# Programs without a block, and another PSUM bank for the fifth unit of the first matmul

## The chip, the cores and the metric

The kernel runs on one core of a Trainium2 chip. A core has five engines that run their own instruction streams and meet only through semaphores: TensorE (PE, with its weight loads shown as PEld), VectorE (DVE), ScalarE (ACT), GpSimd (POOL) and SyncE (SP). SP only starts transfers and waits here; ACT also starts some. The metric is device time in microseconds for one execution. Three runs of the kernel before gave 151.83, 151.93 and 152.18, median 151.93.

## The reference

Two branches are computed on the same input x (2048 rows of 512 in bf16) and mixed by a gate for each row:

```
g = sigmoid((x * gate_w).sum(-1))
A: qkv = x @ wqkv, in 32 heads of 16
   phi(p) = [softmax(p @ w_phi), softmax(-(p @ w_phi))]      per head, for q and for k
   kv = sum over rows of phi_k^T v,   z = sum over rows of phi_k
   a = (phi_q kv / (phi_q z + 1e-6)) @ wo
B: b = relu(x @ w1) @ w2,             w1: 512 x 1376
out = g * a + (1 - g) * b
```

## The kernel before

**Layout.** All is kept in SBUF, 128 rows to a partition tile. x is needed transposed (`XT`). Its first chunk of 512 rows is loaded plain and turned by TensorE with an identity matrix (`xt..`), and ACT and DVE copy the result out of PSUM (`xe..`: `xe30` is the ACT half of the fourth tile of 128 rows); the other three chunks come through transposing DMAs.

**Branch B.** h = relu(x @ w1) is made transposed, in units `h<chunk>_<k>` of 128 of w1's columns by 512 rows: four matmuls into one PSUM bank (`pe_h`, L396). ACT then writes relu of the bank to `HT` (`rl<chunk>_<k>`, L474), and the bank is free again. The first four units of chunk 0 are made piecewise, as x arrives (`hh..`, `hr..`, L410 and L416). Later `b<m>` (L636) multiplies by w2 for each tile m of 128 rows.

**Branch A.** w_phi is folded into the weights first: `f1_0` to `f1_3` for k and `f0_..` for q are four small matmuls each (`pe_fold`, L374) that multiply the transposed wk or wq (`WT`) by a block-diagonal w_phi (`WBD`). DVE evicts `f1_0` and `f1_2` (`fe1_0`, `fe1_2`, L344), ACT the other two (L342). Then x is projected in jobs `pr_k0`, `pr_k1`, ... (L510), and DVE, POOL and ACT make the softmaxes. `a<m>` (L642) adds the A part to the PSUM bank of `b<m>`, ACT scales the sum (`oe<m>`, L687) and starts the store of it (`st<m>`, L690). The last tile is stored in two parts (L681), the second of them by SP.

**PSUM banks.** There are eight. Turning x uses banks 0 and 1 for tiles 0 and 2, and 6 and 7 for tiles 1 and 3. The four folds for k use banks 0, 1, 6, 7 (`FB`) once the turning has left them. The first four h units use banks 3, 4, 5, 2 (`GB4`), and from the fifth unit on the units go round banks 3, 4, 5 (`HB`).

**Order.** The order of the tasks on each engine is written out by hand in the table `ORDER`, one string per engine. A task waits for the tasks that it depends on through one counting semaphore per engine, and one per DMA. The lines of the table around the change are, for PE and ACT:

```
pe : ... hh3 hr0 hr1 h0_0 h0_1 h0_2 h0_3 h0_4 h0_5 f1_0 f1_1 f1_2 f1_3 h0_6 pr_k0 h0_7 h0_8 pr_k1 ...
act: ... xe30 rl0_0 rl0_1 rl0_3 rl0_2 fe1_1 fe1_3 rl0_5 rl0_4 ev_k0 rl0_8 ...
```

**The program's frame.** A block (`nc.Block()`) holds one function per engine. Entering it puts a branch into each engine's stream, and leaving it another branch to a common end. There, in a closing barrier, every engine drains and reports to POOL, POOL releases all, and each takes the release. The profile shows these instructions at L188. A like barrier at the very start (L740) stands ahead of the block, behind the setting of constants. SP's part ends with waits for the last stores to land, written at L708 and L710.

Of the kernel before, what the change touches and what calls it, by code (L numbers as in the profile page):

```python
# [27 lines left out]
    ),  # L28
    "act": (
# [119 lines left out]
def bass_gated_mix__linear_kernel_hedgehog__dense_activation_relu__prompt_kernel(  # L149
# [17 lines left out]
    NT = S // P  # L167
    ND = D // P
# [12 lines left out]
    NPH, NOM, NOT, NOS = 7, 3, 4, 5  # L181
# [6 lines left out]
    with ExitStack() as es:  # L188
        E = es.enter_context

        def sb(name, shape, dt):
            return E(nc.sbuf_tensor(name, shape, dt))
# [4 lines left out]
        WP = sb("WP", [P, 2, ND, D], BF16)  # L197
# [40 lines left out]
        def psap(off, dims):  # L238
            return ap(PS, EPS, off, dims)

        g = _Graph()
        add = g.add
# [5 lines left out]
            boost=700.0)  # L248
# [32 lines left out]
        def chunk(c):  # L281
            return slice(c * 512, (c + 1) * 512)
# [49 lines left out]
        wbd = [f"wbd{j}" for j in range(ND)]  # L332
# [7 lines left out]
        def evict(name, eng, out_, b, deps, **how):  # L340
            if eng == "act":
                add(name, eng, lambda q: q.activation(out_, PS[:, b, :], ACT.Copy), deps, dur=0.6, **how)  # L342
            else:
                add(name, eng, lambda q: q.tensor_copy(out_, PS[:, b, :]), deps, dur=0.69, **how)  # L344

        XB, FB = ((0, 1), (6, 7), (0, 1), (6, 7)), (0, 1, 6, 7)
# [7 lines left out]
        for m in range(4):  # L354
# [3 lines left out]
            for n, eng in enumerate(("act", "dve")):  # L358
                xo = XT[:, 2 * n:2 * n + 2, m * P:(m + 1) * P]
                xi = PS[:, XB[m][n], 0:2 * P].rearrange("p (j t) -> p j t", j=2)  # L360
                if eng == "act":
                    add(f"xe{m}{n}", eng, lambda q, o=xo, i=xi: q.activation(o, i, ACT.Copy), (f"xt{m}{n}",), dur=0.35,
                        boost=9000.0 - 10 * m)
                else:
                    add(f"xe{m}{n}", eng, lambda q, o=xo, i=xi: q.tensor_copy(o, i), (f"xt{m}{n}",), dur=0.37,
                        boost=9000.0 - 10 * m)
# [4 lines left out]
        HB = (3, 4, 5)  # L371
        def pe_fold(q, s, j, b):
            for i in range(ND):
                last = q.matmul(PS[:, b, i * P:(i + 1) * P], WT[:, s * ND + i, j * P:(j + 1) * P], WBD[:, i, :],  # L374
                                start=True, stop=True)
            return last

        for j in range(ND):
            b = FB[j]
            war = [f"xe{2 + j // 2}{j % 2}"]  # L380
            add(f"f1_{j}", "pe", lambda q, j=j, b=b: pe_fold(q, 1, j, b), ("wkT", *wbd, *war), dur=0.24,
                boost=1800.0)
            evict(f"fe1_{j}", ("dve", "act")[j % 2], WP[:, 1, j, :], b, (f"f1_{j}",), boost=1800.0)
        units = []
        for c in range(NC):
            units += [("h", c, k) for k in range(KT - 1)]
# [2 lines left out]
            if c == 2:  # L389
                units += [("f", 0, j) for j in range(ND)]  # L390
        freed = {b: () for b in (*HB, 2)}
        w1of = {k: (() if k < 4 else ("w1b",) if k < 8 else ("w1c",)) for k in range(KT)}

        def pe_h(q, c, k, b):
# [5 lines left out]
        def pe_h_tail(q, c, b):  # L400
            m = KREM + 1
            for n in range(4):
                for j in range(ND):
                    last = q.matmul(PS[:, b, n * m:(n + 1) * m], XT[:, j, c * 512 + n * P:c * 512 + (n + 1) * P],  # L404
                                    W1[:, j, (KT - 1) * P:(KT - 1) * P + m], start=(j == 0), stop=(j == ND - 1))
            return last
# [7 lines left out]
        def pe_h_rest(q, k, c0, c1, first):  # L414
            for j in range(ND):
                last = q.matmul(PS[:, GB4[k], c0:c1], W1[:, j, k * P:(k + 1) * P], XT[:, j, c0:c1],  # L416
                                start=(j == 0 and first), stop=(j == ND - 1), skip_group_check=True)
            return last


        GB4 = (*HB, 2)
# [3 lines left out]
        for j in range(1, ND):  # L425
            add(f"hh{j}", "pe", lambda q, j=j: pe_h_first(q, j, 0, 2 * P), (f"xe0{j // 2}", f"xe1{j // 2}", f"w1a{j}", prev), dur=0.44,
                boost=8500.0)
            prev = f"hh{j}"

        for k in range(2):  # L430
            add(f"hr{k}", "pe", lambda q, k=k: pe_h_rest(q, k, 2 * P, 3 * P, True), ("xe20", "xe21", prev), dur=0.22,
                boost=8200.0)
# [6 lines left out]
        def gate(c):  # L439

            s4 = slice(4 * c, 4 * c + 4)
            add(f"ge{c}", "act", lambda q, s4=s4: q.activation(EG[:, s4], GL[:, s4], ACT.Exp), (f"gr{c}",), dur=0.22)
            add(f"gp{c}", "act", lambda q, s4=s4: q.activation(EP[:, s4], EG[:, s4], ACT.Copy, bias=1.0), (f"ge{c}",),
                dur=0.2)
            add(f"go{c}", "dve", lambda q, s4=s4: q.reciprocal(OMG[:, s4], EP[:, s4]), (f"gp{c}",), dur=0.15)

        for n, (kind, a, k) in enumerate(units):
            b = GB4[n] if n < 4 else HB[(n - 4) % len(HB)]
            if kind == "h":
                halved = n < 4  # L450
                deps = [*xof[a], *w1of[k], prev, *freed[b]]
                if k == KT - 1:
                    deps.append("gw")
                    add(f"h{a}_{k}", "pe", lambda q, a=a, b=b: pe_h_tail(q, a, b), deps, dur=0.69)
                    prev = f"h{a}_{k}"
                    hrow = psap(b * 512, [[KREM + 1, 4], [1, KREM]])
                    add(f"rl{a}_{k}", "act", lambda q, a=a, i=hrow: q.activation(
                        HR[:, a % 2, :, 0:KREM], i, ACT.Relu), (prev, f"hx{a - 2}" if a > 1 else None), dur=0.6, boost=RL)
                    add(f"hx{a}", "sp", lambda q, a=a: q.dma_start_transpose(
                        out=HT[:, KT - 1, chunk(a)].rearrange("p (n t) -> p n t", t=P),  # L460
                        in_=HR[:, a % 2, :, :].rearrange("p n k -> p (n k)")),
                        (f"rl{a}_{k}", "hpad"), dur=1.2, lat=1.6, dma=True)
                    add(f"gr{a}", "dve", lambda q, a=a, b=b: q.tensor_scalar(
                        GL[:, 4 * a:4 * a + 4], psap(b * 512 + KREM, [[KREM + 1, 4]]), GATE_LIMIT, -GATE_LIMIT,
                        ALU.min, ALU.max), (prev, f"rl{a}_{k}"), dur=0.2, boost=500.0)
                    freed[b] = (f"rl{a}_{k}", f"gr{a}")
                    gate(a)
                    continue
                add(f"h{a}_{k}", "pe", lambda q, a=a, k=k, b=b, h=halved:
                    pe_h_rest(q, k, (3 if k < 2 else 2) * P, 4 * P, k > 1) if h else pe_h(q, a, k, b),  # L470
                    deps, dur=(0.22 if k < 2 else 0.44) if halved else 0.87,
                    boost=8000.0 if n < 3 else 0.0)
                prev = f"h{a}_{k}"
                add(f"rl{a}_{k}", "act", lambda q, a=a, k=k, b=b: q.activation(  # L474
                    HT[:, k, chunk(a)], PS[:, b, :], ACT.Relu), (prev,), dur=0.6, boost=RL)
                freed[b] = (f"rl{a}_{k}",)
            else:
                deps = ["wqT", *wbd, prev, *freed[b]]
                add(f"f{a}_{k}", "pe", lambda q, a=a, k=k, b=b: pe_fold(q, a, k, b), deps, dur=0.24, boost=1000.0)
                prev = f"f{a}_{k}"  # L480
                evict(f"fe{a}_{k}", FE, WP[:, a, k, :], b, (prev,), boost=1000.0)
                freed[b] = (f"fe{a}_{k}",)


        VLAG = 4
        widths = [2] * (NT // 2 - 1) + [1, 1]
# [7 lines left out]
        for m in range(NT):  # L494
            def add(*a, boost=20.0 * (len(widths) * 2 - m // 2 - VLAG), **how):
                return g.add(*a, boost=boost, **how)
# [18 lines left out]
        for jn, (kind, tiles) in enumerate(jobs):  # L515
            w = len(tiles)
            n = kind_n[kind]
# [34 lines left out]
            war = [(f"kv{m}" if jobs[jn - NF][0] == "k" else f"tq{m}") for m in jobs[jn - NF][1]] if jn >= NF else []  # L552
# [24 lines left out]
            else:  # L577
# [4 lines left out]
                    dur=0.11 + 0.207 * w)  # L582
# [24 lines left out]
                for m in tiles:  # L607
                    for hf in range(2):
# [10 lines left out]
                        war = [f"o{u0 // 2}_{u0 % 2}"] if u0 >= 0 else [f"ve{NT - 1}"]  # L619
# [26 lines left out]
                    war = [f"oe{m - len(AB)}"] if m >= len(AB) else [f"ve{NT - 1}"] if ab == 2 else list(freed[ab])  # L646
                    if m == NT - 1:
# [15 lines left out]
                        for h2 in range(2):  # L663
                            b, cs = hb[h2], cols[h2]
# [12 lines left out]
                            else:  # L677
                                add(f"oe{m}_1", "dve", lambda q, m=m, b=b, cs=cs: q.tensor_scalar(
                                    OSB[:, m % NOS, cs], PS[:, b, 0:cs.stop - cs.start], OMG[:, m:m + 1], None, ALU.mult), need,
                                    dur=0.4)  # L680
# [14 lines left out]
        order = g.schedule()  # L695
        g.number(order)
        sems = {e: nc.alloc_semaphore(f"s_{e}") for e in ENGINES}
        for t in g.tasks.values():
            if t.dma:
                sems[t.sem] = nc.alloc_semaphore(f"d_{t.name}")  # L700
        block = E(nc.Block())

        @block.sync
        def _(q):
            g.emit("sp", q, order, sems)

            for m in range(NT - NOS - 2, NT - 1):
                q.wait_ge(sems[f"st{m}"], 16)  # L708
            for hf in range(2):
                q.wait_ge(sems[f"st{NT - 1}_{hf}"], 16)  # L710

        @block.gpsimd
        def _(q):
            g.emit("pool", q, order, sems)

        @block.scalar
        def _(q):
            g.emit("act", q, order, sems)

        @block.vector  # L720
        def _(q):
            g.emit("dve", q, order, sems)

        @block.tensor
        def _(q):
            g.emit("pe", q, order, sems)


# [26 lines left out]
```

## Time and profile before

| | |
|---|---|
| timed runs | 151.83, 151.93, 152.18 us (median 151.93) |
| profiled execution, its own time | 150.82 us |
| its span, first to last instruction | 148.9 us (148.94) |
| time around the span | 1.88 us |
| PE busy | 144.6 us, 97% |
| DVE, POOL, ACT busy | 111.0, 109.6, 91.9 us |
| granted TensorE clock | 1.0 |
| last store issued by SP | at 146.73, landing 1.7 us later |

A profile comes from one execution. The timed runs are other executions, and the profiled one was 1.11 us shorter than their median. In the lines of the profile, times are microseconds from the start of the span; L636 is line 636 of the kernel; `PS<-W,HT` is output and inputs by the program's names; `[0.83 <-PE PS L416]` is the idle time of the engine before the group and what ended it. A `q` behind an engine's name marks its sequencer: semaphore, branch, drain and DMA-issuing instructions, which don't count as busy. In the rows of one source line, `17/22/28, 147.2 to 147.2` are the shortest, median and longest duration in ns, and the first and last start in us. Matmuls are pipelined, so that one's row (379 ns) is longer than the distance between two starts (216 ns), and a few matmul rows are missing from the trace.

### The profile page before, as it was taken

To read this page: it belongs to the slowest core of one execution; us is meant where nothing else is said; L and a number is where in the kernel's file an instruction comes from. 1 tells how busy PE (TensorE), PEld (TensorE's weight loads), DVE (VectorE), ACT (ScalarE), POOL (GpSimd) and SP (SyncE) were. 2 spreads that over 40 slices of the span, in tenths; PEclk is the share of its full clock that TensorE was granted. 3 is DMA by queue.
4 is the path that set the end of the run, shared out by engine and by line. 5 is a ranking of instruction groups with operands and counts; after the bars stand their busy time and mean duration, and the time that the engine had idled before them with its cause. 6 is when DMAs were issued, how large, how long until landed. Compare 5 with 4: busy or idle time off the path is not lost.

```text
span 148.9 us, 2614 instructions
## 1 busy us (share of the span) xinstructions
PE 144.6 (97%) x992; PEld 75.3 (51%) x1009; DVE 111.0 (74%) x168; ACT 91.9 (62%) x127; POOL 109.6 (74%) x72
## 2 busy tenths in 40 slices
PE   7999999999999999999999999999999999999992
PEld 2874444445654475445444554455544454455461
DVE  2532667999896948989999997999999969436301
ACT  3457769799969767898983927366565551310151
POOL 4000599999999999999999999999999791240000
DMA  4999999920030001000000191649677585966552
GB/s 149 302 205 190 220 215 193 349 71 4 12 61 0 0 4 37 0 4 0 0 0 0 36 147 35 141 106 142 153 160 198 128 213 106 143 171 146 51 167 69
DMA packets 46364, 16.11 MB, mean 108 GB/s; under 512 B 39856, under 2 KB 46352, under 8 KB 46352
## 3 DMA queue, kind: packets, MB, share of 16 engines
q1 hardware_dynamic: 43616, 13.50, 43.5%
q10 hardware_dynamic: 2736, 2.45, 5.3%
q8 instruction: 8, 0.13, 0.4%
q14 instruction: 4, 0.03, 0.1%
HBM read 4.41 MB, written 2.10 MB: 44 GB/s over the span
## 4 chain that ended last, share of the span: by engine, by line
PE 96%; ACT 1%; issue 1%; DVE 0%
PE PS L636 24%; PE PS L396 21%; PE PS L510 18%; PE PS L490 9%; PE PS L642 9%; PE PS L571 3%; PE PS L614 3%; PE PS L404 2%; PE PS L258 2%; PE PS L657 2%; PE PS L410 1%; PE PS L374 1%; PE PS L350 1%; ACT HT L474 1%; PE PS L668 1%
## 5 line engine op out<-in xcount | busy, mean ns | idle before, releaser
L550 POOL TENSOR_TENSOR TS<-PB,MX 128x1024 bf16<-128x1024 bf16 (+1 forms) x18 | 30.9, 1722 | 14.3 <-DVE MX L541 14.3
L557 DVE TENSOR_REDUCE ZB<-FT 128x128 f32<-128x2048 bf16 (+1 forms) x18 | 36.6, 2032 | 1.8 <-ACT FT L555 1.8
L636 PE MATMUL PS<-W,HT 128*128 128x512 bf16 (+1 forms) x160 | 37.5, 379 | 0.3
L555 ACT ACTIVATE FT<-TS 128x2048 bf16<-128x2048 bf16 (+1 forms) x18 | 30.9, 1718 | 8.7 <-POOL TS L550 8.5
L396 PE MATMUL PS<-XT,W 128*128 128x512 bf16 x141 | 34.3, 379 | 0.2
L550 POOL TENSOR_TENSOR TS<-MN,PB 128x1024 bf16<-128x1024 bf16 (+1 forms) x18 | 30.9, 1724 | 0.8 <-DVE MN L543 0.8
L510 PE MATMUL PS<-WP,XT 128*128 128x512 bf16 x124 | 29.9, 379 | 0.2
L564 POOL TENSOR_TENSOR FT<-FT,SC 128x2048 bf16<-128x2048 bf16 (+1 forms) x9 | 29.5, 3288 | 0.0
L474 ACT ACTIVATE HT<-PS 128x512 bf16<-128x512 f32 x40 | 22.6, 597 | 5.5 <-PE PS L396 4.6
L636 PEld LDWEIGHTS PS<-W,HT 128*128 128x128 bf16 (+1 forms) x165 | 15.5, 98 | 17.1
L541 DVE TENSOR_REDUCE MX<-PB 128x64 bf16<-128x1024 bf16 (+1 forms) x18 | 19.5, 1085 | 6.0 <-ACT PB L537 6.0
L687 ACT ACTIVATE OSB<-PS,OMG 128x512 bf16<-128x512 f32 x15 | 10.2, 687 | 22.3 <-PE PS L642 22.2
L543 DVE TENSOR_REDUCE MN<-PB 128x64 bf16<-128x1024 bf16 (+1 forms) x18 | 19.3, 1084 | 3.2 <-ACT PB L537 3.2
L396 PEld LDWEIGHTS PS<-XT,W 128*128 128x128 bf16 x144 | 13.8, 98 | 15.3
L537 ACT ACTIVATE PB<-PS 128x1024 bf16<-128x1024 f32 (+1 forms) x18 | 16.7, 927 | 6.8 <-PE PS L510 3.7
L510 PEld LDWEIGHTS PS<-WP,XT 128*128 128x128 bf16 x128 | 12.0, 98 | 13.6 <-DVE WP L344 0.4
L587 POOL TENSOR_TENSOR FT<-FT,SR 128x1024 bf16<-128x1024 bf16 (+1 forms) x9 | 15.6, 1739 | 0.7
L490 PE MATMUL PS<-WV,XT 128*128 128x512 bf16 x61 | 15.8, 379 | 0.2
L642 PE MATMUL PS<-WO,OT 128*128 128x512 bf16 x58 | 14.3, 379 | 0.1
L623 DVE SCALAR_TENSOR_TENSOR OTM<-PS,EG,RD 128x256 bf16<-128x256 f32 x32 | 13.8, 463 | 0.4 <-DVE RD L621 0.2
L621 DVE RECIPROCAL RD<-PS 128x16 f32<-128x16 f32 x32 | 6.4, 232 | 8.9 <-PE PS L614 8.7
L499 ACT ACTIVATE VS<-PS 128x512 bf16<-128x512 f32 x16 | 9.6, 602 | 4.3 <-PE PS L490 4.3
(54 smaller groups left out, 104.9 us busy)
## 6 DMA issues: line engine op xcount, KB each, us to landing
out_dram<-OSB ACTq DMA_DIRECT2D x15, 128.0 KB, 2.1
W<-in_B_w_dram SPq DMA_DIRECT2D x1, 1280.0 KB, 7.0
W<-in_B_w_dram SPq DMA_DIRECT2D x1, 512.0 KB, 5.1
WV<-in_A_wqkv_dram SPq DMA_DIRECT2D x1, 512.0 KB, 4.5
WO<-in_A_wo_dram SPq DMA_DIRECT2D x1, 512.0 KB, 7.4
FT<-in_A_x_dram SPq DMA_DIRECT2D x3, 128.0 KB, 3.7
W<-in_B_w_dram SPq DMA_DIRECT2D x1, 352.0 KB, 3.7
W<-in_B_w_dram ACTq DMA_DIRECT2D x2, 128.0 KB, 3.5
```

Source lines behind the costliest of these rows:

```text
L396: last = q.matmul(PS[:, b, :], W1[:, j, k * P:(k + 1) * P], XT[:, j, chunk(c)], start=(j == 0), stop=(j == ND - 1))
L474: add(f"rl{a}_{k}", "act", lambda q, a=a, k=k, b=b: q.activation(HT[:, k, chunk(a)], PS[:, b, :], ACT.Relu), (prev,), dur=0.6, boost=RL)
L490: last = q.matmul(PS[:, 2, :], XT[:, j, m * P:(m + 1) * P], WV[:, j, :], start=(j == 0), stop=(j == ND - 1))
L510: last = q.matmul(PS[:, n, :], XT[:, j, m * P:(m + 1) * P], WP[:, s, j, :], start=(j == 0), stop=(j == ND - 1))
L541: add(f"mx_{J}", "dve", lambda q, sl=sl, w=w, i=pbg: q.tensor_reduce(MX[:, sl, 0:w * H], i, AX.X, ALU.max), (f"ev_{J}", old("t1")), dur=0. ...
L543: add(f"mn_{J}", "dve", lambda q, sl=sl, w=w, i=pbg: q.tensor_reduce(MN[:, sl, 0:w * H], i, AX.X, ALU.min), (f"ev_{J}", old("t2")), dur=0. ...
L550: add(f"{tn}_{J}", "pool", lambda q, o3=o3, a3=a3, b3=b3: q.tensor_tensor(o3, a3, b3, ALU.subtract), (f"{'mx' if sg == 0 else 'mn'}_{J}", ...
L555: add(f"ex_{J}", "act", lambda q, fs=fs, ts=ts, w=w: q.activation(FT[:, fs, 0:w * F], TS[:, ts, 0:w * F], ACT.Exp), (f"t1_{J}", f"t2_{J}", ...
L557: add(f"sm_{J}", "dve", lambda q, fs=fs, sl=sl, w=w: q.tensor_reduce(ZB[:, sl, 0:2 * w * H], FT[:, fs, 0:w * F].rearrange("p (g d) -> p g ...
L564: add(f"nm_{J}", "pool", lambda q, f3=f3, sl=sl, w=w: q.tensor_tensor(f3, f3, SC[:, sl, 0:2 * w * H].unsqueeze(2).to_broadcast([P, 2 * w * ...
L636: last = q.matmul(PS[:, ab, :], HT[0:r, k, m * P:(m + 1) * P], W2[0:r, k, :], start=(k == 0), stop=False)
L642: last = q.matmul(PS[:, ab, :], OT[:, m % NOT, t, :], WO[:, t, :], start=False, stop=(t == ND - 1))
```

## The change

Two things are changed.

First, the block is gone. The tasks of each engine are emitted straight into the main program, and so the branch into the block, the branch out of it and the closing barrier aren't there. SP's waits for the last stores stay, and are its last instructions.

Second, unit `h0_4` writes bank 6 in place of bank 3. It now waits for `xe30`, which empties that bank of x, and no longer for `rl0_0`. The fold `f1_2`, which uses the same bank next, waits for `rl0_4`; for that `rl0_4` is moved ahead of `fe1_1` on ACT. The definition of the folds moves down in the text, since it now refers to `rl0_4`; the order of PE's tasks is the same. `h0_7`, the next unit on bank 3, waits for `rl0_0` and not for `rl0_4`.

```diff
     "act": (
-        "x01 w1a1 w1a3 xe00 xe10 xe20 xe30 rl0_0 rl0_1 rl0_3 rl0_2 fe1_1 fe1_3 rl0_5 rl0_4 ev_k0 rl0_8 rl0_6 "
+        "x01 w1a1 w1a3 xe00 xe10 xe20 xe30 rl0_0 rl0_1 rl0_3 rl0_2 rl0_4 fe1_1 fe1_3 rl0_5 ev_k0 rl0_8 rl0_6 "
...
         freed = {b: () for b in (*HB, 2)}
+        freed[FB[2]] = ("xe30",)
...
-            b = GB4[n] if n < 4 else HB[(n - 4) % len(HB)]
+            b = GB4[n] if n < 4 else FB[2] if n == 4 else HB[(n - 4) % len(HB)]
...
         for j in range(ND):
             b = FB[j]
-            war = [f"xe{2 + j // 2}{j % 2}"]
+            war = [f"xe{2 + j // 2}{j % 2}"] + (["rl0_4"] if j == 2 else [])
             add(f"f1_{j}", "pe", lambda q, j=j, b=b: pe_fold(q, 1, j, b), ("wkT", *wbd, *war), dur=0.24,
                 boost=1800.0)
             evict(f"fe1_{j}", ("dve", "act")[j % 2], WP[:, 1, j, :], b, (f"f1_{j}",), boost=1800.0)
...
-        block = E(nc.Block())
-
-        @block.sync
-        def _(q):
-            g.emit("sp", q, order, sems)
-
-            for m in range(NT - NOS - 2, NT - 1):
-                q.wait_ge(sems[f"st{m}"], 16)
-            for hf in range(2):
-                q.wait_ge(sems[f"st{NT - 1}_{hf}"], 16)
-
-        @block.gpsimd
-        def _(q):
-            g.emit("pool", q, order, sems)
...
+        for e, q in (("sp", nc.sync), ("pool", nc.gpsimd), ("act", nc.scalar), ("dve", nc.vector), ("pe", nc.tensor)):
+            g.emit(e, q, order, sems)
+
+        for m in range(NT - NOS - 2, NT - 1):
+            nc.sync.wait_ge(sems[f"st{m}"], 16)
+        for hf in range(2):
+            nc.sync.wait_ge(sems[f"st{NT - 1}_{hf}"], 16)
```

More of the change, by code (lines that the diff above doesn't have):

```diff
@@ L376, in pe_fold @@
             return last
-        for j in range(ND):
-            b = FB[j]
-            war = [f"xe{2 + j // 2}{j % 2}"]
-            add(f"f1_{j}", "pe", lambda q, j=j, b=b: pe_fold(q, 1, j, b), ("wkT", *wbd, *war), dur=0.24,
-                boost=1800.0)
-            evict(f"fe1_{j}", ("dve", "act")[j % 2], WP[:, 1, j, :], b, (f"f1_{j}",), boost=1800.0)
         units = []
@@ L482, in bass_gated_mix__linear_kernel_hedgehog__dense_activation_relu__prompt_kernel @@
                 freed[b] = (f"fe{a}_{k}",)
+        for j in range(ND):
+            b = FB[j]
+            war = [f"xe{2 + j // 2}{j % 2}"] + (["rl0_4"] if j == 2 else [])
+            add(f"f1_{j}", "pe", lambda q, j=j, b=b: pe_fold(q, 1, j, b), ("wkT", *wbd, *war), dur=0.24,
+                boost=1800.0)
+            evict(f"fe1_{j}", ("dve", "act")[j % 2], WP[:, 1, j, :], b, (f"f1_{j}",), boost=1800.0)
         VLAG = 4
@@ L700, in bass_gated_mix__linear_kernel_hedgehog__dense_activation_relu__prompt_kernel @@
                 sems[t.sem] = nc.alloc_semaphore(f"d_{t.name}")
-        block = E(nc.Block())
-        @block.sync
-        def _(q):
-            g.emit("sp", q, order, sems)
-            for m in range(NT - NOS - 2, NT - 1):
-                q.wait_ge(sems[f"st{m}"], 16)
-            for hf in range(2):
-                q.wait_ge(sems[f"st{NT - 1}_{hf}"], 16)
-        @block.gpsimd
-        def _(q):
-            g.emit("pool", q, order, sems)
[L716 to L726, printed above, removed]
+        for e, q in (("sp", nc.sync), ("pool", nc.gpsimd), ("act", nc.scalar), ("dve", nc.vector), ("pe", nc.tensor)):
[4 more added lines that the diff above has]
+            nc.sync.wait_ge(sems[f"st{NT - 1}_{hf}"], 16)
 _INS = ['A_x', 'A_wqkv', 'A_w_phi', 'A_wo', 'B_x', 'B_w1', 'B_w2', 'gate_w']
```

## The prediction

> **What bounds the kernel now.** Read first the busy shares and the chain of work that ended last: they say whether anything but TensorE can matter in the middle.
>
> ```profile
> span 148.9 us, 2614 instructions
> PE 144.6 (97%) x992; PEld 75.3 (51%) x1009; DVE 111.0 (74%) x168; ACT 91.9 (62%) x127; POOL 109.6 (74%) x72
> PE 96%; ACT 1%; issue 1%; DVE 0%
> ```
>
> TensorE is busy for 144.6 of 148.9 us and is 96% of the chain. Work for TensorE is neither added nor removed by this change, so it can act only where TensorE is idle: about ten microseconds from the start, where the bank is changed, and before the first and after the last instruction of work.
>
> Next, the place of the bank, from the time-ordered lists of ACT and of the weight loads:
>
> ```profile
> 7.84 2.18 ACT L474 ACTIVATE HT<-PS 128x512 bf16<-128x512 f32 x4 [0.83 <-PE PS L416]
> 11.12 1.08 ACT L342 ACTIVATE WP<-PS 128x512 bf16<-128x512 f32 x2 [1.09 <-PE PS L374]
> 12.09 1.09 ACT L474 ACTIVATE HT<-PS 128x512 bf16<-128x512 f32 x2
> ...
> 8.20 0.43 PEld L416 LDWEIGHTS PS<-XT,W 128*128 128x128 bf16 x4
> 8.63 1.50 PEld L396 LDWEIGHTS PS<-XT,W 128*128 128x128 bf16 x8
> 10.37 0.70 PEld L374 LDWEIGHTS PS<-WBD,WT 128*128 128x128 bf16 x11 [0.23 <-DMA WT<-in_A_wqkv_dram]
> ```
>
> The four ACT passes from 7.84 are the evictions rl0_0, rl0_1, rl0_3, rl0_2; the two at 12.09 are rl0_5 and rl0_4. The loads at L396 from 8.63 are h0_4 and h0_5, those at L374 the folds f1_0 to f1_3. No idle time stands before h0_4.
>
> Last, both ends: the rows of the opening (L740) and closing (L188) barriers, and what SyncE waited for.
>
> ```profile
> L740 SPq EVENT_SEMAPHORE  x1: 17/17/17, 0.7 to 0.7; - x1
> L740 PEldq EVENT_SEMAPHORE  x1: 51/51/51, 0.7 to 0.7; - x1
> ...
> 0.74 0.40 SPq L272 DMA_DIRECT2D FT<-in_A_x_dram  x1
> 0.74 0.14 PEld L258 LDWEIGHTS PS<-const-bfloat16-1.0 128*128 128x128 bf16 x2 [0.74 <-issue]
> ...
> 146.73 0.37 SPq L681 DMA_DIRECT2D out_dram<-OSB  x1
> ...
> L710 SPq EVENT_SEMAPHORE  x2: 28/28/28, 148.3 to 148.5; - x2
> ...
> L188 SPq COMPARE_BRANCH  x1: 33/33/33, 148.6 to 148.6; - x1
> L188 SPq DRAIN  x1: 7/7/7, 148.7 to 148.7; - x1
> L188 SPq EVENT_SEMAPHORE  x1: 17/17/17, 148.9 to 148.9; - x1
> ...
> SPq L710 <- DMA out_dram<-OSB: 1.1, 1, 1.1
> SPq L188 <- PEq L188: 0.2, 1, 0.2
> ```
>
> The last store is issued at 146.73 and lands 1.7 us later, at 148.47. After that landing comes only SyncE's last wait for it (148.5), its branch out of the block (148.6), its drain (148.7) and the barrier's release (148.9). Every other engine had been in its own closing drain for a time: ACT, the latest of them, since 147.0. So the stretch behind the landing is on the path of the end, and nothing lies beside it.
>
> **The change, part by part.**
>
> *1. The closing barrier and the branches into it.* In the records behind these rows, read to the nanosecond, SyncE's last wait ends at 148.52 and the span at 148.94: 0.42 us, of which the branch and the gap to the drain are 0.20 (148.52 to 148.72) and the barrier 0.22 (drain, POOL's collection and release, each engine's release). All of it goes: in the changed program SyncE ends with the same four wait instructions and nothing stands behind them. The drains of PE, DVE, ACT and POOL, up to 1757 ns on PE, lay beside SyncE's wait and are worth nothing. Bounds: 0 (what comes after the program has a floor that 0.42 us doesn't move) and 0.64 (0.42, and another 0.22 if a like barrier follows the program, the row being this kernel's own, and four of five engines now reach it early). I take 0.42, the measured stretch itself. **-0.42 us.**
>
> *2. The branches at the start.* Five instructions go, one per engine. No row of the trace shows one at the start, where the only branch on record is SyncE's closing one, which carried a wait. Between the end of the barrier's release and the first work there are 25 ns on PE (0.718 to 0.743), 60 on ACT and 65 on SyncE (0.673 to 0.738). So the gain is between 0 and 65 ns. I take 0, since 25 ns on PE leaves little room for a branch and a weight load's issue. In the opening the loads of x set TensorE's pace, so SyncE and ACT are the queues that would count.
> [...]
>
> *3. The fifth unit's bank.* h0_4 (eight matmuls with h0_5 at L396) wrote bank 3 and so waited for rl0_0; it now writes bank 6 and waits for xe30, whose ACT pass ended at 7.01. The old wait had ended by 8.44 (rl0_0 is the first pass from 7.84, 598 ns long), and h0_4's first weights were loaded at 8.63, on the heels of the loads of L416: 0.19 us to spare. Nothing is gained, since TensorE came no later for that wait. Bounds: 0 and a gain of 0.05 us, what an execution could lose whose ACT pass came 0.24 later than this one's (half of a pass). I take 0, as in the row.
>
> *4. What the bank now delays.* f1_2, the third fold, writes bank 6 after h0_4's eviction, so rl0_4 is moved on ACT ahead of fe1_1, fe1_3 and rl0_5, and f1_2 gets a wait on ACT. Queued behind it on PE are f1_2, f1_3, h0_6 and the first projection pr_k0; behind rl0_4 on ACT are fe1_1 and fe1_3, for which pr_k0 waits. The times: rl0_4 can start when h0_4's last matmul is done (9.39 + 0.38 = 9.77, about 0.04 later for the semaphore) and ACT is free after rl0_2. ACT's back-to-back passes start 0.495 apart (8.941, 9.436), so it starts at 9.93 and, 0.60 long, ends at 10.53. f1_2's weights would be loaded at 10.86: the folds begin at 10.47 and f1_2 is the ninth of matmuls 56 ns apart. Spare: 0.33 us. fe1_1 starts at 11.12, when f1_1 is done, so ACT has been idle for 0.55 us by then. Both are covered: cost 0. Bounds: 0, and one ACT pass late (0.495 - 0.33 = 0.17 us).
>
> *5. What rl0_4 leaves.* ACT's second pass in the 1.09 us from 12.09 goes; ACT then waits for pr_k0 until 14.27 anyway. h0_7, which took bank 3 after rl0_4 (13.18), now takes it after rl0_0; it started at 14.07 behind pr_k0. No gain. A stall of 0.10 us before pr_k0 (12.24 to 12.34, waiting for fe1_3 on ACT and fe1_2 on DVE) stays, since the folds keep their times. No DMA, no instruction of POOL and no place in SyncE's queue moves.
>
> **Sum.** -0.42 + 0 + 0 + 0. The profiled execution took 150.82 us: 148.94 of span and 1.88 around it. It becomes 148.52 + 1.88 = 150.40. The median of the timed runs, 151.93, stands 1.11 above the profiled one; I carry that over unchanged: **151.51 us**, 0.28% faster. No change and a change can be told apart at about 0.2% here, 0.30 us.
>
> **The rivals.**
>
> *A. The end isn't shortened (151.93).* What follows the span, 1.88 us that no row opens, might be set by an engine's fixed work and not by SyncE's arrival. For it: the trace shows nothing of that time. Against it: before the change all five engines left the barrier within 50 ns at 148.9, so whatever followed began there, and it can begin earlier now on each. This is also the case where the change does nothing.
>
> *B. More than the barrier goes (151.3).* If the five engines meet once more after the program, four of them now arrive early, and only SyncE's part of that meeting is left. Priced by this kernel's own closing barrier, 0.22 us: 151.51 - 0.22 = 151.29. For it: the drains of the other engines were over by 147.2. Against: the length of the later meeting is unseen.
> [...]
>
> *C. The end waits for its own code (slower).* SyncE now goes straight from its last wait into what follows, 0.42 us sooner. If that code has to be fetched and the barrier gave cover to it, the fetch comes onto the path. Prices from the queues that fetch instructions (packets, MB, share of 16 engines):
>
> ```profile
> q8 instruction: 8, 0.13, 0.4%
> q14 instruction: 4, 0.03, 0.1%
> ```
>
> 0.4% of 16 x 148.9 us over 8 packets is 1.2 us each, 0.1% over 4 is 0.6. A small one gives 151.51 + 0.6 = 152.11, a large one 152.71, 0.5% slower; it decides from 0.72 us on (0.42 + 0.30). Against: the branch at 148.6 reached its target's drain 0.13 us later, so no fetch was waited for even at that jump.
>
> *D. f1_2 is held by rl0_4.* Only a loss beyond 0.42 us shows, so rl0_4 must be 0.75 us late, about one and a half ACT passes. At one pass late the time is 151.51 + 0.17 = 151.68.
>
> **How the numbers follow.** The sum's own case (1 to 5 as taken, within 0.15 us either way from the bounds of parts 2 to 4 and the spread of the runs shown, 151.83 to 152.18) has 0.62. A has 0.17, B 0.13, C 0.05, D 0.03. Faster by over 0.2% needs 151.63 or less: about six sevenths of the sum's case (0.53) and all of B give 0.66. Within 0.2%: the rest of the first (0.09), nearly all of A, all of D and a little of C: 0.29. Slower: the larger price of C and the edge of A, 0.05. The range runs from B's lower side, 151.2, to the upper edge of A, 152.0; outside lie C and a little of A and B, about 0.1.
>
> **What would show it.** Part 1: no row at L188, and a span that ends with SyncE's last wait, at about 148.5, some 2 us after the issue of the last store. Part 2: the first DMA issues and weight load at 0.74 still (0.68 would make it the branch). Parts 3 and 4: h0_4's weight loads without idle time at 8.63, a fifth ACT pass on HT from about 9.93, the folds unbroken from 10.47 and pr_k0 at 12.34. A and B show only in the time around the span: 2.30 in A, 1.66 in B, 1.88 in the sum's case. The forecast is wrong if that time grows by what the span loses, or if a gap opens among the folds.

## The result, and the profile after

| | before | after |
|---|---|---|
| median of 6 runs | 151.68 us | 150.62 us |
| lowest and highest | 151.16 to 152.18 | 150.27 to 150.72 |
| profiled execution, its own time | 150.82 | 150.59 |
| its span | 148.94 | 149.27 |
| time around the span | 1.88 | 1.32 |

The ratio of the times is 0.9934, with a 95% interval of 0.991 to 0.9958. The change is faster by 0.66%, 1.06 us, more than twice what was forecast, and the time lies 0.58 us below the range.

The table holds what surprises: the span of the profiled execution is longer than before, and its time is shorter all the same. The time around the span is the execution's time less its span. It holds what follows the last instruction and whatever of the execution lies ahead of the first; no row divides the two, so it is the difference between kernels that is read. The two halves of the change are best read apart.

*The frame.* These are the first issues of the profile after, the last ones, and the rows of SyncE's last waits (L709 is L710 of before).

```profile
0.74 0.41 ACTq L272 DMA_DIRECT2D FT<-in_A_x_dram  x1
0.74 0.40 SPq L272 DMA_DIRECT2D FT<-in_A_x_dram  x1
0.74 0.14 PEld L258 LDWEIGHTS PS<-const-bfloat16-1.0 128*128 128x128 bf16 x2 [0.74 <-issue]
...
147.39 0.35 ACTq L683 DMA_DIRECT2D out_dram<-OSB  x1
147.49 0.37 SPq L683 DMA_DIRECT2D out_dram<-OSB  x1
...
L709 SPq EVENT_SEMAPHORE  x2: 28/28/28, 149.1 to 149.2; - x2
```

The opening is the same to the hundredth: 0.74 for the first transfers and the first weight load. At the end nothing stands behind L709: no branch, no drain, no release. The record puts the end of the last wait and of the span both at 149.27, where before there were 0.42 us between them. Beyond the span, 1.32 us are left of 1.88. So 0.42 + 0.56 = 0.98 us have gone from the time from SyncE's last wait to the end of the execution, and that is the gain but for 0.08.

*The bank.* ACT and the weight loads around the fifth unit, after:

```profile
8.51 2.67 ACT L469 ACTIVATE HT<-PS 128x512 bf16<-128x512 f32 x5 [0.89 <-PE PS L411]
11.78 1.08 ACT L342 ACTIVATE WP<-PS 128x512 bf16<-128x512 f32 x2 [0.60 <-PE PS L374]
12.75 0.60 ACT L469 ACTIVATE HT<-PS 128x512 bf16<-128x512 f32 x1
...
8.14 1.14 PEld L411 LDWEIGHTS PS<-XT,W 128*128 128x128 bf16 x14
9.30 1.50 PEld L391 LDWEIGHTS PS<-XT,W 128*128 128x128 bf16 x8
10.92 1.10 PEld L374 LDWEIGHTS PS<-WBD,WT 128*128 128x128 bf16 x16
```

A fifth pass joins ACT's first group (2.67 us for 2.18), and ACT's idle time before the evictions of the folds falls from 1.09 to 0.60 us; while some of it is left, those evictions start no later for the fifth pass. The folds' loads are unbroken, though f1_2 among them now waits for ACT.

*Why the span is longer.* All of this comes 0.66 us later than before, and the bank has no part in it, for it begins earlier, at TensorE's first units. Before, and then after: the rows of these matmuls, their stretches on the chain that ended last, and their durations.

```profile
4.29 1.72 PE L410 MATMUL PS<-XT,W 128*128 128x128 bf16 x16
4.46 1.56 PE PS L410 x16
L410 PE MATMUL PS<-XT,W x20: 219/272/314, 4.3 to 6.9; 128*128 128x256 bf16 x12, 128*128 128x128 bf16 x8
```

```profile
4.31 2.49 PE L405 MATMUL PS<-XT,W 128*128 128x128 bf16 x16
4.48 2.33 PE PS L405 x16
L405 PE MATMUL PS<-XT,W x20: 272/314/421, 4.3 to 7.4; 128*128 128x256 bf16 x12, 128*128 128x128 bf16 x8
```

The same sixteen matmuls take 2.33 us on the chain, where they took 1.56, and no wait for a load stands among them in either profile. In the records behind these rows those of 256 columns start 0.11 us apart before, from 4.98 on, and 0.21 apart after, until 6.42. In the profiled execution of after TensorE thus doubled its rate about 1.5 us later. No row shows why: the granted clock reads 1.00 in both, but the one clock record that after has within its span begins at 6.42, just there, and before has none. In other profiles the opening is held by a load. The third piece of w1 that these matmuls need, issued at 1.65 to 1.67 in all fourteen profiles of this study, landed between 4.90 and 6.59 us. In eight of the fourteen the next weights are loaded 0.10 to 0.11 us behind that landing. In the other six it isn't what they wait for: it landed at 4.94 before and at 5.60 after, and with the earliest landing of all, 4.90, `h0_4` still began at 9.39. Over the fourteen profiles h0_4's first weights are loaded between 8.59 and 9.81 us.

The span of one kernel varies by about a microsecond from run to run (before: 148.9 to 150.2 in 28 runs), and one profile against another can't show the change. The time around the span is steadier: 1.76 to 2.05 in those 28 runs, mean 1.90, and 1.28 to 1.37 in six runs of after, mean 1.32. The spans of single runs are on record to 0.1 us, so each of these single values is good to 0.05.

### The profile page after: what moved, and what is told of

Its sections match the earlier page's. It is cut to its first block, busy times and chain, and to the rows that moved or that the text cites. A ratio compares the mean times of both kernels' runs of the same rounds, so it can differ in the third digit from the quotient of the medians.

```text
span 149.3 us, 2619 instructions
## 1 busy us (share of the span) xinstructions
PE 146.3 (98%) x1009; PEld 75.9 (51%) x1009; DVE 110.9 (74%) x168; ACT 91.8 (61%) x127; POOL 109.6 (73%) x72
## 4 chain that ended last, share of the span: by engine, by line
PE 98%; DVE 0%; issue 0%
PE PS L638 24%; PE PS L391 21%; PE PS L512 19%; PE PS L492 9%; PE PS L644 9%; PE PS L573 3%; PE PS L616 3%; PE PS L399 2%; PE PS L405 2%; PE PS L258 2%; PE PS L659 2%; PE PS L411 1%; PE PS L374 1%; PE PS L350 1%; PE PS L670 1%; DVE OSB L680 0%
## 5 line engine op out<-in xcount | busy, mean ns | idle before, releaser
L638 PE MATMUL PS<-W,HT 128*128 128x512 bf16 (+1 forms) x165 | 38.1, 379 | 0.0
L512 PE MATMUL PS<-WP,XT 128*128 128x512 bf16 x128 | 30.6, 379 | 0.0
L492 PE MATMUL PS<-WV,XT 128*128 128x512 bf16 x64 | 16.4, 379 | 0.0
```

The source lines that it names most:

```text
L492: last = q.matmul(PS[:, 2, :], XT[:, j, m * P:(m + 1) * P], WV[:, j, :], start=(j == 0), stop=(j == ND - 1))
L512: last = q.matmul(PS[:, n, :], XT[:, j, m * P:(m + 1) * P], WP[:, s, j, :], start=(j == 0), stop=(j == ND - 1))
L638: last = q.matmul(PS[:, ab, :], HT[0:r, k, m * P:(m + 1) * P], W2[0:r, k, :], start=(k == 0), stop=False)
```

## The experiments

The theory after the result: the closing barrier cost its 0.42 us of span, and in addition it made five engines begin together what each has to do after the program; without it four of them are through by the time SyncE ends. Rivals: the bank carries the rest; or the gain comes from the programs' length, since each engine has fewer instructions and one page of them less to fetch. The number read is the span's part behind SyncE's last wait, from the profile, and the time around the span, a mean over the runs of a kernel. Their sum is called the time from the last wait to the end of the execution, though it holds what lies ahead of the first instruction as well.

**The block alone, and the bank alone.** The first kernel is before with the frame of after; the second is after with the frame of before.

```diff
-        block = E(nc.Block())
...
+        for e, q in (("sp", nc.sync), ("pool", nc.gpsimd), ("act", nc.scalar), ("dve", nc.vector), ("pe", nc.tensor)):
+            g.emit(e, q, order, sems)
```

> The block removed alone; h0_4 stays on bank 3. The changed kernel took 0.42 us less of span behind the last wait, and 0.56 us less around the span (1.32 for 1.88). If all of the change's gain is in the frame: about 1.0 us faster than before (ratio 0.9935), 1.3 us around the span. If the bank carries the rest beyond 0.42: ratio 0.997.

> The bank alone, with the block and its closing barrier kept. If the bank is worth nothing: ratio 1.000, and 1.88 us around the span. If the bank carries half a microsecond: ratio 0.9965, and the time around the span stays 1.88.

Measured: without the block 150.29 us, ratio 0.9928 (0.9909 to 0.9946), and 1.31 us around the span. With the bank alone 151.31 us, ratio 0.9997 (0.9978 to 1.0016), and 1.89 us around. The frame carries the whole gain. The two profiles show the bank's stretch almost side by side, since both executions happened to reach it at the same time. The block removed, with the old bank:

```profile
8.17 2.18 ACT L474 ACTIVATE HT<-PS 128x512 bf16<-128x512 f32 x4 [0.89 <-PE PS L416]
11.44 1.08 ACT L342 ACTIVATE WP<-PS 128x512 bf16<-128x512 f32 x2 [1.09 <-PE PS L374]
...
8.96 1.50 PEld L396 LDWEIGHTS PS<-XT,W 128*128 128x128 bf16 x8
10.58 1.09 PEld L374 LDWEIGHTS PS<-WBD,WT 128*128 128x128 bf16 x16
...
12.64 0.56 PEld L510 LDWEIGHTS PS<-WP,XT 128*128 128x128 bf16 x4 [0.42 <-DVE WP L344]
```

The bank changed, with the block:

```profile
8.16 2.67 ACT L469 ACTIVATE HT<-PS 128x512 bf16<-128x512 f32 x5 [0.88 <-PE PS L411]
11.44 1.08 ACT L342 ACTIVATE WP<-PS 128x512 bf16<-128x512 f32 x2 [0.60 <-PE PS L374]
...
8.95 1.50 PEld L391 LDWEIGHTS PS<-XT,W 128*128 128x128 bf16 x8
10.57 1.09 PEld L374 LDWEIGHTS PS<-WBD,WT 128*128 128x128 bf16 x16
...
12.63 0.56 PEld L512 LDWEIGHTS PS<-WP,XT 128*128 128x128 bf16 x4 [0.42 <-DVE WP L344]
```

h0_4, the folds and pr_k0 start at the same time in both, 0.01 us apart. Neither the wait that went nor the one that came is felt.

**All engines late, without a barrier; and the barrier without a block.**

```diff
         for hf in range(2):
             nc.sync.wait_ge(sems[f"st{NT - 1}_{hf}"], 16)
+        nc.gpsimd.wait_ge(sems[f"st{NT - 1}_1"], 16)
+        nc.scalar.wait_ge(sems[f"st{NT - 1}_1"], 16)
+        nc.vector.wait_ge(sems[f"st{NT - 1}_1"], 16)
+        nc.tensor.wait_ge(sems[f"st{NT - 1}_1"], 16)
```

> The changed kernel, in which PE, ACT, DVE and POOL each end with one wait for the very last store, as SP does: no branch and no barrier, but all five engines end together. If the 0.56 us around the span came from four engines that end early: 1.85 to 1.9 us around the span, the time 0.5 us above the changed kernel's (151.1). If it came from the shorter programs (an instruction page that need not be fetched at the end): 1.3 us around, time as the changed kernel's (150.6).

```diff
             nc.sync.wait_ge(sems[f"st{NT - 1}_{hf}"], 16)
+        nc.all_engine_barrier()
```

> The changed kernel with the closing barrier put back, without the branches. Early ends or program length alike give 1.85 to 1.9 us around the span again. The span's part behind the last wait tells the price of the barrier from that of SP's branch: 0.22 us if the record's split before was right (drain to release), 0.42 if the branch's gap belongs to the barrier.

With all engines late the time is 151.31 us, ratio 0.9992 (0.9974 to 1.0011): no faster than with block and barrier. Around the span there are 2.09 us, above the 1.85 to 1.9 expected. The added waits as the profile has them, one for each engine:

```profile
L710 POOLq EVENT_SEMAPHORE  x1: 17/17/17, 149.6 to 149.6; - x1
L711 ACTq EVENT_SEMAPHORE  x1: 17/17/17, 149.6 to 149.6; - x1
L712 DVEq EVENT_SEMAPHORE  x1: 21/21/21, 149.6 to 149.6; - x1
L713 PEldq EVENT_SEMAPHORE  x1: 51/51/51, 149.6 to 149.6; - x1
```

With the barrier put back it is 151.23 us, ratio 0.9993 (0.9969 to 1.0018), with 0.26 us of span behind SyncE's last wait (near the 0.22 of the prediction's split) and 1.98 around. Both agree with early ends. The second agrees with the programs' length as well, and the first nearly excludes it, but it has one instruction more on four engines than after. The next run closes that.

**The same length, but early.** The four added waits are for the first load of x, which landed at 3.3 us in this profile.

```diff
+        nc.gpsimd.wait_ge(sems["x00"], 16)
+        nc.scalar.wait_ge(sems["x00"], 16)
+        nc.vector.wait_ge(sems["x00"], 16)
+        nc.tensor.wait_ge(sems["x00"], 16)
```

> The changed kernel, in which PE, ACT, DVE and POOL each end with one wait for the first load of x, which landed at 3.4 us. Each program is as long as in the kernel where all wait for the last store, but the four engines end early. If early ends make the gain: 1.3 us from the last wait to the end of the execution, as in the changed kernel, and a time near 150.5. If one more instruction per program shifts a page that is fetched at the end: 2.1 to 2.2, and 151.3.

Measured: 150.81 us, ratio 0.995 (0.9924 to 0.9977), and 1.33 us around the span. The same four lines, now early:

```profile
L710 POOLq EVENT_SEMAPHORE  x1: 17/17/17, 130.7 to 130.7; - x1
L711 ACTq EVENT_SEMAPHORE  x1: 17/17/17, 147.1 to 147.1; - x1
L712 DVEq EVENT_SEMAPHORE  x1: 21/21/21, 146.4 to 146.4; - x1
L713 PEldq EVENT_SEMAPHORE  x1: 51/51/51, 144.7 to 144.7; - x1
```

The programs are as long as those of the run with all engines late, and only the time at which the four engines end differs: 1.33 (1.27 to 1.39) against 2.09 (1.82 to 2.31). The early ends are shown to be the cause. How they act isn't shown.

**Which engine ends last.** SyncE's waits for the last stores are moved to another engine, as here to ACT, and all others end early.

```diff
-            nc.sync.wait_ge(sems[f"st{m}"], 16)
+            nc.scalar.wait_ge(sems[f"st{m}"], 16)
...
-            nc.sync.wait_ge(sems[f"st{NT - 1}_{hf}"], 16)
+            nc.scalar.wait_ge(sems[f"st{NT - 1}_{hf}"], 16)
```

> The changed kernel with the waits for the last stores on ACT in place of SP; SP then ends at its last issue, 1.4 us sooner. If it matters only how many engines come early: 1.3 us behind the last wait, the time as the changed kernel's. If the order of the engines in what follows matters, it differs: up to 2.1 (all of the gain lost) where ACT stands early in that order, and below 1.3 where it stands late.

> The changed kernel with the waits for the last stores on POOL, which otherwise ends at about 132 us. If only the number of early engines matters: 1.3 us behind the last wait. If the order matters, it differs from 1.3, between under 1.3 and 2.1.

> The changed kernel with the waits for the last stores on DVE, which otherwise ends at about 147 us. If only the number of early engines matters: 1.3 us behind the last wait. If the order matters, it differs from 1.3, between under 1.3 and 2.1.

> The changed kernel with the waits for the last stores on PE. So far the time from the last wait to the end of the execution was 1.32 us with SP last, 1.45 DVE, 1.78 ACT, 1.87 POOL, and 2.09 with all five last. If what follows passes through the engines in a fixed order and the first in it costs all of it: PE gives about 2.1. If the five add up in part: PE gives less, 1.3 to 1.9.

| engine that ends last | mean around the span, us (range over the runs) | time, us | ratio to before |
|---|---|---|---|
| SyncE (the changed kernel) | 1.32 (1.28 to 1.37) | 150.62 | 0.9934 (0.991 to 0.9958) |
| DVE | 1.45 (1.39 to 1.50) | 150.67 | 0.9939 (0.9911 to 0.9966) |
| PE | 1.58 (1.54 to 1.63) | 150.54 | 0.9947 (0.9914 to 0.998) |
| ACT | 1.78 (1.73 to 1.85) | 151.06 | 0.9959 (0.9936 to 0.9982) |
| POOL | 1.87 (1.82 to 1.91) | 151.2 | 0.9976 (0.9953 to 1.0) |

Of the ranges around the span only those of ACT and POOL overlap (1.82 to 1.85). The ratios are each to runs of before taken beside them, and their intervals are too wide to give the order of the rows; it is read from the second column. Who ends last matters by up to 0.55 us, where all together cost 0.77 more than SyncE alone, and SyncE, where the waits already stood, is the cheapest of the five. With POOL alone late four engines come early too, and around the span there is as much as before (1.87 and 1.90), so the number of early engines doesn't decide by itself. That PE would give about 2.1, as the first in a fixed order, was a miss: it gives 1.58, and no engine alone reaches the 2.09 of all together.

**Pairs and groups.** One line of the run with all engines late is kept, or one is left out.

```diff
+        nc.scalar.wait_ge(sems[f"st{NT - 1}_1"], 16)
```

> The changed kernel in which ACT alone also waits for the last store, so that SP and ACT end last together. If the costliest of the late engines sets the end: 1.78 us, as with ACT alone. If each late engine adds its part to SP's 1.32: 1.78 plus something.

```diff
+        nc.gpsimd.wait_ge(sems[f"st{NT - 1}_1"], 16)
```

> The changed kernel in which POOL alone also waits for the last store. If the costliest late engine sets the end: 1.87 us, as with POOL alone. If the parts add: more, up to the 2.09 of all five.

```diff
+        nc.scalar.wait_ge(sems[f"st{NT - 1}_1"], 16)
+        nc.vector.wait_ge(sems[f"st{NT - 1}_1"], 16)
+        nc.tensor.wait_ge(sems[f"st{NT - 1}_1"], 16)
```

> The changed kernel in which PE, ACT and DVE also wait for the very last store, and POOL alone ends early (at about 132 us). With SP and POOL last the time behind the last wait was 2.23, with all five 2.09, with SP and ACT 1.72, with SP alone 1.32. If POOL's early end carries the gain: 1.3 to 1.5 and a time near 150.6. If any late engine beside SP costs about as much: 1.7 to 1.8, near 151.1. If POOL's end is worth nothing once the others are late: 2.1.

Measured around the span: SyncE with ACT 1.72 (1.43 to 1.96), with POOL 2.23 (1.86 to 2.33), with PE, ACT and DVE but not POOL 1.90 (1.53 to 2.10). The times are 150.98, 151.41 and 151.14 us, the ratios 0.9961 (0.9935 to 0.9987), 0.9996 (0.9964 to 1.0028) and 0.9979 (0.9955 to 1.0003). Neither rule fits all three. POOL and SyncE together cost more than POOL alone and, in the mean, more than all five, so it isn't the costliest engine that sets the end; POOL's early end alone saves 0.19 of 0.77, so POOL doesn't carry it either. In each of these three the runs spread over 0.47 to 0.57 us, and with all engines late over 0.49, where a lone last engine stayed within 0.12. What each engine does after its program, and in what order they meet, stays open: no row of a trace here covers it.

## Why the prediction was right and wrong, point by point

**The step that failed is the one from span to time** in part 1 and the sum: 1.88 us around the span, "148.52 + 1.88 = 150.40". The reading of the span in part 1 was right: the stretch of 0.42 us behind the last wait went whole. But the 1.88 were carried over as if nothing behind the program depended on when the engines end, and they became 1.32. The upper bound of 0.64 for the whole part was too low for the same reason, as 0.98 went.

**Rival B was the right mechanism at the wrong size.** It said that four engines now come early to whatever follows, and priced that at 0.22 us, the length of this kernel's own closing barrier. Means over runs give 1.90 - 1.32 = 0.58. The price was taken from a row where the engines only meet, and that it would hold for what comes behind the program was assumed; what follows the program costs 0.77 us more with all five late (2.09) than with SyncE alone late (1.32).

The accounting of the microsecond, from SyncE's last wait to the end of the execution:

| | behind the wait, in the span | around the span | sum | difference |
|---|---|---|---|---|
| before, with branch and barrier | 0.42 | 1.90 | 2.32 | |
| barrier without branches | 0.26 | 1.98 | 2.24 | -0.08 |
| no barrier, all engines late | 0.04 | 2.09 | 2.13 | -0.11 |
| no barrier, SyncE late | 0 | 1.32 | 1.32 | -0.81 |

So the branch and the barrier by themselves were worth some 0.2 us, not 0.42: without them, but with five engines ending together, half of what the span loses comes back around it (0.38 and 0.19), and the time is before's (0.9992). The 0.42 of the sum is right as a stretch of the span, but as the price of branch and barrier alone it is about twice too large. The large step, 0.81, goes with the early ends of the other four engines, for which the sum had nothing. The two small steps, 0.08 and 0.11, are less than the spread of single runs (1.81 to 2.09 and 1.82 to 2.31 around the span), and the parts in the span are from one profile each.

**The base.** The prediction started from 151.93, the median of three runs; six gave 151.68, and the 13 to 29 runs beside the experiments 151.38 to 151.57. Of the miss of 0.89 us (151.51 to 150.62), 0.25 is the base and 0.58 the time around the span.

**Part 2** (no gain at the start) was right: 0.74 us for the first issues in both, and no branch stands there in either trace.

**Parts 3 to 5** (the bank is worth nothing either way) were right: 0.9997, and the two profiles in step to 0.01 us. The spare of 0.33 us that was worked out for f1_2 is there after: ACT's fifth pass ended at 11.18, and f1_2's first weights, the ninth of the folds' loads, went in at 11.52 with no gap among them. ACT's idle time behind that pass is 0.60 us; the prediction's own times give 11.12 - 10.53 = 0.59, and not the 0.55 that it wrote.

**Rival A** (no gain) fell with the time itself, though its mechanism shows in part in the run with all engines late: 0.38 us of the span are gone there, and 0.19 come back around it. **C** (code to fetch on the path of the end) doesn't show: the time around the span fell. But a fetch stands near the end in six of the fourteen profiles, one packet on an instruction queue, 1.75 to 2.21 us behind the last wait: before, the bank alone, all engines late, the barrier put back, SyncE with POOL, and POOL alone early. It is absent after and in the other seven:

```profile
q14 instruction: 1, 0.01, 1.2%
```

This row is of before, for the window from 149.5 us on. The profiles with it are those whose time from the last wait to the end is 1.93 us or more, and those without it have 1.86 or less. With POOL alone last there are 1.86 us and no fetch, against 1.32 with SyncE, so the fetch isn't what makes one late engine dearer than another. Whether it is part of the price when several end together, or only falls where the end comes late enough, stays open. **D** (f1_2 held) fell with the bank's runs.

**What would show it** was stated rightly for B: a shorter time around the span. It came out below all three values that were named for it (2.30, 1.88 and 1.66). The forecast for the span, 148.5, rested on one execution with a quick opening; it was 149.27.

## What to carry to other kernels

The time around the span was shorter here when the other engines had ended early (1.33 us and not 2.09), so leave out a closing barrier where the last engine's own waits already cover the outputs. Let one engine end last, and choose which: here it was 1.32 us with SyncE and 1.87 with POOL. And read the time around the span beside the span in each run, for a change at the very end can hide there (0.58 us here), while the span of one execution moved by a microsecond (148.9 to 150.2 in 28 runs of before).

## What was not expected of the hardware

- The time around the span differed with the engine that ended last: SyncE 1.32, DVE 1.45, PE 1.58, ACT 1.78, POOL 1.87 us, each within 0.12 us over 6 to 10 runs.
- The dearest ends were those of engines that ended together: five engines 2.09 us, SyncE and POOL alone 2.23 (single runs 1.82 to 2.31 and 1.86 to 2.33).
- The branch into the block cost nothing measurable at the start: the first transfers are issued at 0.74 us with it and without it.
- The same 128 KB load, issued at 1.65 to 1.67 us, landed between 4.90 and 6.59 us in fourteen profiles, and in eight of them TensorE's first units went on 0.10 to 0.11 us behind it.
